# VectorE's low parts, empty-row constants and logits' running sum as instructions of one scalar and two tensors, with new emission times for all steps

## The chip, the core and the metric

The kernel runs on one core of one Trainium2 chip. A core has five engines that run side by side, each through its own queue in order: TensorE (PE in the profile; its weight loads are PEld), VectorE (DVE), ScalarE (ACT), GpSimd (POOL) and SyncE (SP), which here only issues DMA transfers. The metric is the device time of one execution in microseconds (us). The kernel before took 521.79 us (median of 3 runs, 521.64 to 521.96).

## What is computed

Attention with buckets: 4 batches of 8 heads, 768 positions, 64 dimensions a head. Each query and key gets a bucket from the signs of six projections, and a query sees only the keys of its own bucket. A mixture of experts of the soft kind follows: 32 slots, 8 experts, weights of 2 x 16.8 MB.

```python
q_bits = (np.einsum('bhsd,dk->bhsk', q, proj) > 0)
k_bits = (np.einsum('bhsd,dk->bhsk', k, proj) > 0)
mask = q_bucket[:, :, :, None] == k_bucket[:, :, None, :]
scores = np.where(mask, scale * q @ k.T, -1e9)
attn = exp(scores - max) / (sum + 1e-9)
x = attn @ v                                  # 3072 x 512
logits = x @ phi                              # 3072 x 32
d = softmax of logits over the rows           # weighs x into 32 slots
slot_out = relu(slot_input @ w1) @ w2         # four slots an expert
out = softmax of logits over the slots @ slot_out
```

A row whose query finds no key of its bucket has all scores equal, and so becomes the mean of v.

## The kernel before

The 32 heads are handled in pairs, and one pair is one period of the work. `split_hi` (ScalarE) and `split_lo` (L285, VectorE from head 4 on, GpSimd before) split queries and keys of a pair into a rounded part and the rest, the low part: low = raw - high, 128 partitions by 768, twice a pair. The parts are brought by DMA into two operands X and Y of each head (`spread_x`, `spread_y`, `spread_l`), and the sign bits, found by `bits` on TensorE and VectorE, into rows of the same operands (`spread_bits`).

For each head, `smax` multiplies twelve pieces of bits and rounded parts on TensorE into a PSUM tile of 512 columns (`smx`, two buffers), and VectorE takes the row maxima (L367, L370). The twelve pieces are of 512 and 256 columns in turn; two pieces of 256 share a tile. `shift` (L372) makes from the maxima, three small VectorE instructions one after the other, the numbers that are subtracted: L376 the maximum of a row, L377 a huge constant for rows in which nothing matches, L379 the shift itself. `shift_rows` (L383) turns them on TensorE (L386), copies them on ScalarE, and a DMA ("mr") puts them into a row of the operands. `scores` (L393) does the full product on TensorE, two matmuls a piece, into a tile of `st` (three buffers), and ScalarE takes exps into `pts` (L406). GpSimd adds these up in `acc` (five sums of 128x768 a head, L413 and L419), and `av` (L421) multiplies them with v on TensorE, 24 matmuls in a row.

For each pair, `pair_sum`, `pair_turn`, `pair_rec`, `pair_log`, `pair_add` (L461) and `pair_x` make the reciprocals of the sums, the logits and the rows of x. `pair_add` multiplies the pair's logits (L469) and adds them to a running sum over the four pairs of a batch (L471). The `batch_` steps once a batch do the softmax over rows in running form. After the last head comes the tail: the experts and the output, in which most of the weights are read.

The order of all instructions is written out in the kernel: each step has an emission time in a table, `STEADY` for what comes back every pair and `ONCE` for single steps. One unit, a slot, is a twelfth of a pair's period. The times only sort: `at` puts each step on a list with its pair's start (12 slots a pair) added, the list is sorted, and steps are emitted one after the other. Each engine, and SP's queue, then runs its part of that order; an instruction that waits holds up everything behind it on its engine. A key such as `('smax', 1, 5, 0)` names the step, the head in the pair (0 even, 1 odd) and its piece, so 14.0 in the table is slot 2.0 of the next pair. Weight pieces of 512 KB are loaded between, by `load_weights`.

Of the kernel before, what the change touches and what calls it, by code (L numbers as in the profile page):

```python
# [991 lines left out]
```

## Time and profile before

| | us |
|---|---|
| median of 3 runs | 521.79 |
| profiled execution | 522.49 |
| its span | 520.5 |
| one period (pair of heads) in the middle | 26.40 |
| tail, from 461 us on | 59.0 |

The profile shows one execution. Its first part gives the busy time of each engine and its share of the span, then come the chain of work that ended last, and the costliest groups of instructions. A group's row has the line, engine and operation, what is written from what, its shape and count, then the busy time in us, the mean of one in ns, and after the second bar how long the engine had been idle before, and what ended that. In rows of the waits stand the engine and line that waited, whom it waited for, and us in total, number of times, and the longest. In rows of the timeline stand the start and duration in us; a bracket gives the idle time before it and what ended it. Matmuls are pipelined: each is shown until its last column is out, while the next has begun, so a busy TensorE is not one at its peak.

### The profile page before, as it was taken

To read this page: it belongs to the slowest core of one execution; us is meant where nothing else is said; L and a number is where in the kernel's file an instruction comes from. 1 tells how busy PE (TensorE), PEld (TensorE's weight loads), DVE (VectorE), ACT (ScalarE), POOL (GpSimd) and SP (SyncE) were. 2 spreads that over 40 slices of the span, in tenths; PEclk is the share of its full clock that TensorE was granted. 3 is DMA by queue.
4 is the path that set the end of the run, shared out by engine and by line. 5 is a ranking of instruction groups with operands and counts; after the bars stand their busy time and mean duration, and the time that the engine had idled before them with its cause. 6 is when DMAs were issued, how large, how long until landed. Compare 5 with 4: busy or idle time off the path is not lost.

```text
span 520.5 us, 8938 instructions
## 1 busy us (share of the span) xinstructions
PE 482.5 (93%) x3155; PEld 293.3 (56%) x3155; DVE 411.6 (79%) x699; ACT 248.1 (48%) x462; POOL 336.4 (65%) x226
## 2 busy tenths in 40 slices
PE   6879899999999999999999999999999998969992
PEld 4446465656565665656555656565656565453562
DVE  4736889999998899999988999999979966544333
ACT  4044546454646464636473646464745454412232
POOL 9247859595958786867677886868678959301200
PEclk9569999999999999999999999999999999989997
DMA  3758565757565657676766676766766576779967
GB/s 104 175 104 209 152 169 140 189 124 201 117 193 117 197 123 211 151 209 151 200 156 185 169 199 169 199 168 175 188 163 173 135 206 223 290 285 369 410 270 287
DMA packets 39801, 99.60 MB, mean 191 GB/s; under 512 B 7470, under 2 KB 13756, under 8 KB 39756
## 3 DMA queue, kind: packets, MB, share of 16 engines
q1 hardware_dynamic: 38956, 97.37, 65.7%
q10 hardware_dynamic: 608, 1.57, 1.4%
q8 instruction: 25, 0.41, 0.3%
q14 instruction: 20, 0.16, 0.1%
q0 software_dynamic: 192, 0.08, 0.1%
HBM read 52.76 MB, written 6.29 MB: 113 GB/s over the span
## 4 chain that ended last, share of the span: by engine, by line
PE 78%; DVE 12%; DMA 3%; issue 2%; SPq 1%; ACT 1%; POOL 0%; DVEq 0%; POOLq 0%; ACTq 0%
PE st L402 23%; PE av L430 22%; PE smx L364 13%; DVE mz L377 4%; PE qs L915 3%; PE qh L833 3%; DVE mx L370 3%; PE mi L457 2%; PE av L237 2%; PE mi L492 2%; DVE w L287 2%; PE mi L321 2%; DMA XY<-w 2%; PE mi L386 1%; SPq L291 1%
## 5 line engine op out<-in xcount | busy, mean ns | idle before, releaser
L419 POOL TENSOR_TENSOR acc<-acc,pt 128x768 f32<-128x768 f32 x125 | 243.8, 1950 | 13.7 <-ACT pt L406 5.1
L406 ACT ACTIVATE pt<-st 128x512 f32<-128x512 f32 x288 | 166.8, 597 | 54.3 <-PE st L402 46.3
L402 PE MATMUL st<-XY 128*128 128x256 f32 (+1 forms) x768 | 184.2, 349 | 2.7 <-DMA XY<-mr 2.7
L370 DVE TENSOR_REDUCE mx<-smx 128x1 f32<-128x512 f32 x192 | 126.8, 681 | 19.5 <-PE smx L364 17.1
L402 PEld LDWEIGHTS st<-XY 128*128 128x128 f32 x768 | 124.9, 192 | 26.4 <-issue 9.0
L430 PE MATMUL av<-pt,v 128*64 128x384 f32 x768 | 130.9, 490 | 0.0
L364 PE MATMUL smx<-XY 96*128 96x512 f32 (+1 forms) x384 | 122.3, 369 | 8.7 <-DVE mx L370 3.0
L413 POOL TENSOR_TENSOR acc<-pt 128x768 f32<-128x768 f32 x32 | 58.4, 1824 | 65.3 <-ACT pt L406 64.8
L430 PEld LDWEIGHTS av<-pt,v 128*64 128x64 f32 x768 | 52.3, 137 | 76.1 <-issue 75.5
L364 PEld LDWEIGHTS smx<-XY 96*128 96x128 f32 x384 | 68.3, 194 | 30.1 <-DVE mx L370 14.6
L367 DVE TENSOR_REDUCE mx<-smx 128x2 f32<-128x512 f32 x96 | 64.4, 683 | 7.9 <-PE smx L364 7.7
L434 ACT COPY avs<-av 128x384 f32<-128x384 f32 x32 | 15.3, 479 | 113.9 <-PE av L430 113.9
L287 DVE TENSOR_TENSOR w<-raw,w 128x768 fp32r<-128x768 f32 x28 | 57.1, 2069 | 1.5 <-ACT w L283 1.5
L449 DVE RECIPROCAL sm<-sm 128x128 f32<-128x128 f32 x45 | 38.3, 907 | 0.0
L283 ACT CAST w<-raw 128x768 fp32r<-128x768 f32 x32 | 25.0, 830 | 8.7 <-DMA v<-vt 7.8
L377 DVE TENSOR_SCALAR mz<-m 128x6 f32<-128x6 f32 x32 | 25.4, 792 | 1.2
L494 DVE TENSOR_TENSOR xq<-mi,r 128x256 f32<-128x256 f32 x45 | 17.4, 414 | 6.1 <-PE mi L492 6.1
L386 PE MATMUL mi<-ident,mz 128*128 128x128 f32 x32 | 9.7, 304 | 10.9 <-DVE mz L379 10.8
L471 DVE TENSOR_TENSOR lacc<-lacc,sm 128x384 f32<-128x384 f32 x11 | 17.4, 1582 | 0.4
L386 PEld LDWEIGHTS mi<-ident,mz 128*128 128x128 f32 x32 | 4.5, 140 | 22.6 <-DVE mz L379 19.1
L389 ACT CAST mr<-mi 12x128 fp32r<-12x128 f32 x32 | 7.8, 245 | 19.5 <-PE smx L364 11.1
L492 PEld LDWEIGHTS mi<-ident,avs 128*128 128x128 f32 x90 | 10.5, 140 | 10.4 <-issue 8.4
(168 smaller groups left out, 356.7 us busy)
## 6 DMA issues: line engine op xcount, KB each, us to landing
w<-w SPq DMA_DIRECT2D x61, 512.0 KB
XY<-w SPq DMA_DIRECT2D x61, 384.0 KB
raw<-qk SPq DMA_DIRECT2D x32, 384.0 KB
XY<-w SPq DMA_DIRECT2D x60, 192.0 KB
v<-vt SPq DMA_DIRECT2D x32, 192.0 KB
out<-w SPq DMA_DIRECT2D x12, 512.0 KB
xq<-w SPq DMA_DIRECT2D x3, 512.0 KB
XY<-bt SPq DMA_DIRECT2D x62, 19.5 KB
```

The costliest lines, as they stand in the source:

```text
L283: nc.scalar.copy(w[:, 2 * x], st[h]["raw"][:, x])
L287: (nc.vector if h > 2 else nc.gpsimd).tensor_tensor(out=w[:, 2 * x + 1], in0=st[h]["raw"][:, x], in1=w[:, 2 * x], op=ALU.subtract)
L364: nc.tensor.matmul(pt[:, o:o + b - a], Ys[h % N_Y][0:96, 0, t * P:(t + 1) * P], Ys[h % N_Y][0:96, 1, a:b], start=True, stop=True)
L367: nc.vector.tensor_reduce(out=mx[:, n - 1:n + 1], in_=pt.rearrange("p (a x) -> p a x", a=2), axis=AX.X, op=ALU.max)
L370: nc.vector.reduce_max(out=mx[:, n:n + 1], in_=pt, axis=AX.X)
L377: nc.vector.tensor_scalar(out=mz[:, NT:2 * NT], in0=m, scalar1=NOMATCH, scalar2=BIG, op0=ALU.is_lt, op1=ALU.mult)
L402: nc.tensor.matmul(pt[:, o:o + b - a], x[:, 1, i * P:(i + 1) * P], x[:, 0, a:b], start=first, stop=not first)
L406: nc.scalar.activation(pts[i // 2][:, 512 * u:512 * u + 512], pt, AF.Exp, scale=D ** -0.5)
L413: nc.gpsimd.tensor_tensor(out=s["acc"], in0=pr[:, 0:S], in1=pr[:, S:2 * S], op=ALU.add)
L419: eng.tensor_tensor(out=s["acc"], in0=s["acc"], in1=pr[:, a * S:(a + 1) * S], op=ALU.add)
L430: nc.tensor.matmul(s["av"][64 * c:64 * c + 64, 0:HC], s["v"][:, i, :], pr[:, o + c * HC:o + (c + 1) * HC], start=(i == 0), stop=(i == NT - 1))
L449: nc.vector.reciprocal(out=rs[:, k * P:(k + 1) * P], in_=rs[:, k * P:(k + 1) * P])
```

## The change

Three VectorE instructions become `scalar_tensor_tensor`, which computes (in0 op0 scalar) op1 in1. The low part, a `tensor_tensor`, becomes raw x 1.0 - high for the heads where VectorE does it. The constant of empty rows, a `tensor_scalar` with two scalars, becomes (m < NOMATCH) x bigs, with `bigs` a new tile of 128x6 that holds the constant BIG and is filled once. The running sum of the logits becomes product x 1.0 + sum.

The emission times of `STEADY` are new for all steps but those of the batches, and of `ONCE` those of the weight pieces 5 to 16. The last loop's bound is written so that it takes in the last time of the plan.

```diff
@@ -43,32 +43,36 @@
 
 
 STEADY = {
-    ('acc', 0, 0): 4.9176, ('acc', 0, 1): 5.0337, ('acc', 0, 2): 6.1361, ('acc', 1, 0): 9.6777,
-    ('acc', 1, 1): 12.1046, ('acc', 1, 2): 14.8971, ('av', 0, 0): 4.8805, ('av', 0, 1): 5.7492,
-    ('av', 0, 2): 5.7838, ('av', 1, 0): 11.6706, ('av', 1, 1): 11.6874, ('av', 1, 2): 11.7943,
+    ('acc', 0, 0): 0.91143595, ('acc', 0, 1): 3.17478349, ('acc', 0, 2): 3.59676867, ('acc', 1, 0): 10.88626624,
+    ('acc', 1, 1): 11.33964379, ('acc', 1, 2): 11.82064114, ('av', 0, 0): 4.078226, ('av', 0, 1): 4.27318607,
+    ('av', 0, 2): 4.47578804, ('av', 1, 0): 11.29101187, ('av', 1, 1): 11.30451101, ('av', 1, 2): 11.80872392,
     ('batch_both',): 20.1, ('batch_exp',): 23.0, ('batch_max',): 22.4, ('batch_scale',): 24.396,
     ('batch_share',): 27.6, ('batch_slots',): 26.173, ('batch_turn',): 23.9, ('batch_weigh',): 24.65,
-    ('bits', 0): -13.9515, ('load', 0): -21.3522, ('load_v', 0): -1.8154, ('load_v', 1): 5.7068,
-    ('pair_add', 0): 17.5916, ('pair_log', 0): 16.8678, ('pair_rec', 0, 0): 16.4953, ('pair_rec', 0, 1): 17.1338,
-    ('pair_rec', 0, 2): 16.9038, ('pair_sum', 0): 15.349, ('pair_turn', 0): 16.3852, ('pair_x', 0, (0, 1)): 21.8276,
-    ('pair_x', 0, (2,)): 17.8398, ('scores', 0, 0, 0): 0.9834, ('scores', 0, 0, 1): 2.5325,
-    ('scores', 0, 1, 0): 2.9425, ('scores', 0, 1, 1): 2.5183, ('scores', 0, 2, 0): 1.1584,
-    ('scores', 0, 2, 1): -0.0074, ('scores', 0, 3, 0): 0.2266, ('scores', 0, 3, 1): 2.0502,
-    ('scores', 0, 4, 0): 3.0286, ('scores', 0, 4, 1): 3.0745, ('scores', 0, 5, 0): 3.6791,
-    ('scores', 0, 5, 1): 4.2554, ('scores', 1, 0, 0): 7.8115, ('scores', 1, 0, 1): 5.8647,
-    ('scores', 1, 1, 0): 6.6763, ('scores', 1, 1, 1): 9.4999, ('scores', 1, 2, 0): 7.9254,
-    ('scores', 1, 2, 1): 9.9037, ('scores', 1, 3, 0): 9.9177, ('scores', 1, 3, 1): 6.8119,
-    ('scores', 1, 4, 0): 7.1407, ('scores', 1, 4, 1): 8.2097, ('scores', 1, 5, 0): 9.8883,
-    ('scores', 1, 5, 1): 9.6186, ('shift', 0): -3.963, ('shift', 1): 2.6162, ('shift_rows', 0): -2.4189,
-    ('shift_rows', 1): 3.4038, ('smax', 0, 0, 0): -8.8298, ('smax', 0, 0, 1): -8.0218, ('smax', 0, 1, 0): -7.8723,
-    ('smax', 0, 1, 1): -4.9963, ('smax', 0, 2, 0): -4.1493, ('smax', 0, 2, 1): -4.8002, ('smax', 0, 3, 0): -4.4071,
-    ('smax', 0, 3, 1): -8.7934, ('smax', 0, 4, 0): -5.8528, ('smax', 0, 4, 1): -5.6775, ('smax', 0, 5, 0): -5.2739,
-    ('smax', 0, 5, 1): -7.6138, ('smax', 1, 0, 0): -2.3741, ('smax', 1, 0, 1): -3.9733, ('smax', 1, 1, 0): -3.7428,
-    ('smax', 1, 1, 1): -2.0923, ('smax', 1, 2, 0): -2.0138, ('smax', 1, 2, 1): 1.7604, ('smax', 1, 3, 0): 2.4338,
-    ('smax', 1, 3, 1): 0.8492, ('smax', 1, 4, 0): 0.923, ('smax', 1, 4, 1): -3.663, ('smax', 1, 5, 0): -2.5459,
-    ('smax', 1, 5, 1): 2.5831, ('split_hi', 0): -14.0129, ('split_lo', 0, 0): -13.788, ('split_lo', 0, 1): -12.9073,
-    ('spread_bits', 0): -10.5295, ('spread_bits', 1): -6.4877, ('spread_l', 0): -6.9257, ('spread_l', 1): -5.2234,
-    ('spread_x', 0): -9.4685, ('spread_x', 1): -5.2165, ('spread_y', 0): -13.7846, ('spread_y', 1): -7.1185,
+    ('bits', 0): -13.95890534, ('load', 0): -21.84228255, ('load_v', 0): -1.51318162, ('load_v', 1): 4.63191299,
+    ('pair_add', 0): 15.99028816, ('pair_log', 0): 15.89036858, ('pair_rec', 0, 0): 15.31234319,
+    ('pair_rec', 0, 1): 15.74808174, ('pair_rec', 0, 2): 15.83774187, ('pair_sum', 0): 14.25462034,
+    ('pair_turn', 0): 14.78228382, ('pair_x', 0, (0, 1)): 21.81002444, ('pair_x', 0, (2,)): 16.53595504,
+    ('scores', 0, 0, 0): 0.42937858, ('scores', 0, 0, 1): 0.10975419, ('scores', 0, 1, 0): 0.37566801,
+    ('scores', 0, 1, 1): 0.06354472, ('scores', 0, 2, 0): 2.73608952, ('scores', 0, 2, 1): 0.39545741,
+    ('scores', 0, 3, 0): 1.17190303, ('scores', 0, 3, 1): 2.96375079, ('scores', 0, 4, 0): 0.91043595,
+    ('scores', 0, 4, 1): 1.58215641, ('scores', 0, 5, 0): 2.32865234, ('scores', 0, 5, 1): 2.43752751,
+    ('scores', 1, 0, 0): 6.82167698, ('scores', 1, 0, 1): 5.28419876, ('scores', 1, 1, 0): 5.49659969,
+    ('scores', 1, 1, 1): 5.70056921, ('scores', 1, 2, 0): 9.5088345, ('scores', 1, 2, 1): 6.24519176,
+    ('scores', 1, 3, 0): 6.27277748, ('scores', 1, 3, 1): 9.83928317, ('scores', 1, 4, 0): 9.71651955,
+    ('scores', 1, 4, 1): 7.80253627, ('scores', 1, 5, 0): 9.44600188, ('scores', 1, 5, 1): 7.50325885,
+    ('shift', 0): -2.89738435, ('shift', 1): 2.67478786, ('shift_rows', 0): -2.14833088,
+    ('shift_rows', 1): 3.02147361, ('smax', 0, 0, 0): -7.00077299, ('smax', 0, 0, 1): -8.63468468,
+    ('smax', 0, 1, 0): -8.20918051, ('smax', 0, 1, 1): -6.29379503, ('smax', 0, 2, 0): -5.39311908,
+    ('smax', 0, 2, 1): -6.75745749, ('smax', 0, 3, 0): -6.47510133, ('smax', 0, 3, 1): -4.73315438,
+    ('smax', 0, 4, 0): -8.59086819, ('smax', 0, 4, 1): -4.27385444, ('smax', 0, 5, 0): -4.25336427,
+    ('smax', 0, 5, 1): -3.26636443, ('smax', 1, 0, 0): 2.40118286, ('smax', 1, 0, 1): -2.02963968,
+    ('smax', 1, 1, 0): -2.01736929, ('smax', 1, 1, 1): 0.30153939, ('smax', 1, 2, 0): 0.03611274,
+    ('smax', 1, 2, 1): 1.34851447, ('smax', 1, 3, 0): 1.74922724, ('smax', 1, 3, 1): 2.09633042,
+    ('smax', 1, 4, 0): 2.28076515, ('smax', 1, 4, 1): -2.41700748, ('smax', 1, 5, 0): -2.06779907,
+    ('smax', 1, 5, 1): 0.84522444, ('split_hi', 0): -14.12691859, ('split_lo', 0, 0): -13.3249754,
+    ('split_lo', 0, 1): -13.04048452, ('spread_bits', 0): -13.92314133, ('spread_bits', 1): -8.21018051,
+    ('spread_l', 0): -4.89960371, ('spread_l', 1): -6.85974162, ('spread_x', 0): -10.40239078,
+    ('spread_x', 1): -7.05038, ('spread_y', 0): -11.52688803, ('spread_y', 1): -8.46779598,
 }
 
 ONCE = {
@@ -78,24 +82,24 @@
...
-    ('load_weights', 14): 129.5946, ('load_weights', 15): 135.9087, ('load_weights', 16): 141.5946,
...
-    ('load_weights', 5): 75.9087, ('load_weights', 6): 81.5946, ('load_weights', 7): 87.9087,
...
+    ('load_weights', 13): 118.272186073, ('load_weights', 14): 124.277596692, ('load_weights', 15): 130.272186073,
+    ('load_weights', 16): 136.277596692, ('load_weights', 17): 153.5946, ('load_weights', 18): 156.8062,
...
+    ('load_weights', 4): 63.9087, ('load_weights', 5): 70.272186073, ('load_weights', 6): 76.277596692,
...
@@ -195,6 +199,8 @@
 
     eps = cp.tile([P, 1], F32, name="eps")
     nc.vector.memset(eps, EPS)
+    bigs = cp.tile([P, NT], F32, name="bigs")
+    nc.vector.memset(bigs, BIG)
     ones = cp.tile([P, 32], F32, name="ones")
     nc.vector.memset(ones, 1.0)
     idle = pts[2][:, 0:P]
@@ -284,7 +290,12 @@
 
     def split_lo(h, x):
         w = st[h]["w4"]
-        (nc.vector if h > 2 else nc.gpsimd).tensor_tensor(out=w[:, 2 * x + 1], in0=st[h]["raw"][:, x], in1=w[:, 2 * x], op=ALU.subtract)
+        raw = st[h]["raw"][:, x]
+        if h > 2:
+            nc.vector.scalar_tensor_tensor(out=w[:, 2 * x + 1], in0=raw, scalar=1.0, in1=w[:, 2 * x],
+                                           op0=ALU.mult, op1=ALU.subtract)
+        else:
+            nc.gpsimd.tensor_tensor(out=w[:, 2 * x + 1], in0=raw, in1=w[:, 2 * x], op=ALU.subtract)
 
     def move(dst, src, eng=nc.sync):
 
@@ -374,8 +385,8 @@
         mz = mzp
         m = mp.tile([P, NT], F32, name="m", bufs=1)
         nc.vector.tensor_reduce(out=m, in_=s["mx"], axis=AX.X, op=ALU.max)
-        nc.vector.tensor_scalar(out=mz[:, NT:2 * NT], in0=m, scalar1=NOMATCH, scalar2=BIG,
-                                op0=ALU.is_lt, op1=ALU.mult)
+        nc.vector.scalar_tensor_tensor(out=mz[:, NT:2 * NT], in0=m, scalar=NOMATCH, in1=bigs,
+                                       op0=ALU.is_lt, op1=ALU.mult)
         nc.vector.scalar_tensor_tensor(out=mz[:, 0:NT], in0=m, scalar=-1.0, in1=mz[:, NT:2 * NT],
                                        op0=ALU.mult, op1=ALU.subtract)
         s["mz"] = mz
@@ -468,7 +479,8 @@
             dst = st[h]["rs"]
         nc.vector.tensor_tensor(out=dst, in0=pt[:, 0:HC], in1=st[h]["rs"], op=ALU.mult)
         if g:
-            nc.vector.tensor_tensor(out=lacc_of[b], in0=lacc_of[b], in1=dst, op=ALU.add)
+            nc.vector.scalar_tensor_tensor(out=lacc_of[b], in0=dst, scalar=1.0, in1=lacc_of[b],
+                                           op0=ALU.mult, op1=ALU.add)
 
     def pair_turn(h):
         sm = st[h]["sm"]
@@ -773,7 +785,7 @@
         at(load_weights, wa, 1, tag=n)
 
     plan.sort(key=lambda w: w[:2])
-    for slot in range(int(plan[0][0] // 1), last + 5):
+    for slot in range(int(plan[0][0] // 1), max(last + 5, int(plan[-1][0]) + 1)):
         if slot == last - 14:
             free_pp()
             wb = ctx.enter_context(tc.tile_pool(name="wb", bufs=N_WB))
```

More of the change, by code (lines that the diff above doesn't have):

```diff
@@ L85 @@
-    ('load_weights', 2): 39.9087, ('load_weights', 20): 168.8062, ('load_weights', 21): 177.5946,
-    ('load_weights', 22): 189.5946, ('load_weights', 3): 51.9087, ('load_weights', 4): 63.9087,
-    ('load_weights', 5): 75.9087, ('load_weights', 6): 81.5946, ('load_weights', 7): 87.9087,
-    ('load_weights', 8): 93.5946, ('load_weights', 9): 99.9087, ('one_add', 30): 190.708, ('one_add', 31): 193.725,
-    ('one_fold', 3): 189.992, ('one_log', 30): 188.431, ('one_log', 31): 193.725, ('one_put', 30): 192.78,
@@ L90 @@
-    ('one_put', 31): 195.725, ('one_rec', 30): 190.438, ('one_rec', 31): 193.725, ('one_sum', 30): 189.395,
-    ('one_sum', 31): 193.725, ('one_turn', 30): 189.777, ('one_turn', 31): 193.725, ('one_x', 30): 191.23,
-    ('one_x', 31): 193.725, ('smax', 1, 0, 0): -2.3, ('smax', 1, 0, 1): -2.29, ('smax', 1, 1, 0): -2.28,
-    ('smax', 1, 1, 1): -2.1, ('smax', 1, 2, 0): -2.05, ('smax', 1, 2, 1): -2.0, ('smax', 1, 3, 0): -1.99,
-    ('smax', 1, 3, 1): -1.9, ('smax', 1, 4, 0): -1.8, ('smax', 1, 4, 1): 0.62, ('smax', 1, 5, 0): 0.63,
@@ L95 @@
-    ('smax', 1, 5, 1): 1.2, ('split_hi', 2): -1.5, ('split_lo', 2, 0): -1.45, ('split_lo', 2, 1): -1.44,
-    ('spread_bits', 1): -7.869, ('spread_bits', 2): 0.4, ('spread_l', 0): -12.047, ('spread_l', 1): -12.02,
-    ('spread_l', 2): 0.5, ('spread_x', 0): -12.04, ('spread_x', 1): -12.03, ('spread_x', 2): 0.6,
-    ('spread_y', 1): -14.012, ('spread_y', 2): -1.2,
+    ('load_phi',): -7.0, ('load_weights', 0): 16.4515, ('load_weights', 1): 27.9087,
+    ('load_weights', 10): 100.277596692, ('load_weights', 11): 106.272186073, ('load_weights', 12): 112.277596692,
@@ new lines @@
+    ('load_weights', 13): 118.272186073, ('load_weights', 14): 124.277596692, ('load_weights', 15): 130.272186073,
+    ('load_weights', 16): 136.277596692, ('load_weights', 17): 153.5946, ('load_weights', 18): 156.8062,
+    ('load_weights', 19): 165.5946, ('load_weights', 2): 39.9087, ('load_weights', 20): 168.8062,
+    ('load_weights', 21): 177.5946, ('load_weights', 22): 189.5946, ('load_weights', 3): 51.9087,
+    ('load_weights', 4): 63.9087, ('load_weights', 5): 70.272186073, ('load_weights', 6): 76.277596692,
@@ new lines @@
+    ('load_weights', 7): 82.272186073, ('load_weights', 8): 88.277596692, ('load_weights', 9): 94.272186073,
+    ('one_add', 30): 190.708, ('one_add', 31): 193.725, ('one_fold', 3): 189.992, ('one_log', 30): 188.431,
+    ('one_log', 31): 193.725, ('one_put', 30): 192.78, ('one_put', 31): 195.725, ('one_rec', 30): 190.438,
+    ('one_rec', 31): 193.725, ('one_sum', 30): 189.395, ('one_sum', 31): 193.725, ('one_turn', 30): 189.777,
+    ('one_turn', 31): 193.725, ('one_x', 30): 191.23, ('one_x', 31): 193.725, ('smax', 1, 0, 0): -2.3,
@@ new lines @@
+    ('smax', 1, 0, 1): -2.29, ('smax', 1, 1, 0): -2.28, ('smax', 1, 1, 1): -2.1, ('smax', 1, 2, 0): -2.05,
+    ('smax', 1, 2, 1): -2.0, ('smax', 1, 3, 0): -1.99, ('smax', 1, 3, 1): -1.9, ('smax', 1, 4, 0): -1.8,
+    ('smax', 1, 4, 1): 0.62, ('smax', 1, 5, 0): 0.63, ('smax', 1, 5, 1): 1.2, ('split_hi', 2): -1.5,
+    ('split_lo', 2, 0): -1.45, ('split_lo', 2, 1): -1.44, ('spread_bits', 1): -7.869, ('spread_bits', 2): 0.4,
+    ('spread_l', 0): -12.047, ('spread_l', 1): -12.02, ('spread_l', 2): 0.5, ('spread_x', 0): -12.04,
@@ L99 @@
+    ('spread_x', 1): -12.03, ('spread_x', 2): 0.6, ('spread_y', 1): -14.012, ('spread_y', 2): -1.2,
 }
```

3 lines of the change are left out of this document (removed).

## The prediction

> **What bounds the kernel now.** I read the page first, then the table of windows, the waits, and the timeline of one period. The page:
>
> ```profile
> span 520.5 us, 8938 instructions
> PE 482.5 (93%) x3155; PEld 293.3 (56%) x3155; DVE 411.6 (79%) x699; ACT 248.1 (48%) x462; POOL 336.4 (65%) x226
> PE 78%; DVE 12%; DMA 3%; issue 2%; SPq 1%; ACT 1%; POOL 0%; DVEq 0%; POOLq 0%; ACTq 0%
> ```
>
> TensorE is busy 93% and makes 78% of the chain that ended last; VectorE's 12% is what can be taken out. One period is two heads, 12 slots of the plan. Its row in the table of windows:
>
> ```profile
> core 0: us, PE busy (x) PEld busy (x) DVE busy (x) ACT busy (x) POOL busy (x), PEclk, DMA share, GB/s
> 112.70:139.10 26.40, 25.48 (x156) 15.74 (x156) 24.90 (x37) 13.82 (x26) 19.44 (x11) 1.00 0.63 161
> ...
> 461.00:520.00 59.00, 49.46 (x547) 28.68 (x547) 21.36 (x75) 15.59 (x34) 6.03 (x32) 0.93 0.82 323
> ```
>
> In 26.40 us TensorE stands still for 0.92 us, at full clock; VectorE is busy for 24.90. The last row, the tail, is little touched by the change. The waits name the standstill, and the timeline shows one:
>
> ```profile
> PE mi L386 <- DVE mz L379: 10.8, 12, 1.3
> ```
>
> ```profile
> 113.66 0.69 DVE L370 TENSOR_REDUCE mx<-smx 128x1 f32<-128x512 f32 x1 [0.23 <-PE smx L364]
> ...
> 114.38 0.17 DVE L376 TENSOR_REDUCE m<-mx 128x6 f32<-128x12 f32 x1
> ...
> 114.57 1.81 POOL L413 TENSOR_TENSOR acc<-pt 128x768 f32<-128x768 f32 x1 [0.19 <-ACT pt L406]
> 114.58 1.83 DVE L377 TENSOR_SCALAR mz<-m 128x6 f32<-128x6 f32 x1
> ...
> 116.45 0.17 DVE L379 SCALAR_TENSOR_TENSOR mz<-m,mz 128x6 f32<-128x6 f32 x1
> 116.46 7.53 POOL L419 TENSOR_TENSOR acc<-acc,pt 128x768 f32<-128x768 f32 x4
> ...
> 116.67 0.33 PE L386 MATMUL mi<-ident,mz 128*128 128x128 f32 x1 [0.86 <-DVE mz L379]
> ```
>
> L377 handles six numbers per partition, yet begins 0.01 us after GpSimd's sum and ends just when that ends. Such a standstill happens in 12 of 32 heads and costs TensorE 10.8 us in all. The other VectorE rows that the change touches:
>
> ```profile
> L287 DVE TENSOR_TENSOR w<-raw,w 128x768 fp32r<-128x768 f32 x28 | 57.1, 2069 | 1.5 <-ACT w L283 1.5
> ...
> L377 DVE TENSOR_SCALAR mz<-m 128x6 f32<-128x6 f32 x32 | 25.4, 792 | 1.2
> ...
> L471 DVE TENSOR_TENSOR lacc<-lacc,sm 128x384 f32<-128x384 f32 x11 | 17.4, 1582 | 0.4
> ...
> L379 DVE SCALAR_TENSOR_TENSOR mz<-m,mz 128x6 f32<-128x6 f32 x32 | 5.3, 166 | 1.1
> ...
> L419 DVE TENSOR_TENSOR acc<-acc,pt 128x768 f32<-128x768 f32 x2 | 1.9, 950 | 0.0
> ...
> L648 DVE SCALAR_TENSOR_TENSOR run_x<-run_x,al,mi 128x512 f32<-128x512 f32 x2 | 1.5, 746 | 3.7 <-PE mi L642 3.7
> ...
> L922 DVE SCALAR_TENSOR_TENSOR w<-w,con,qs 128x256 fp32r<-128x256 f32 x2 | 1.0, 480 | 5.9 <-ACT w L921 5.9
> ...
> L555 DVE TENSOR_TENSOR lacc<-lacc,sm 64x384 f32<-64x384 f32 x1 | 0.6, 551 | 0.0
> ```
>
> A two-tensor sum of 768 columns takes 950 ns where GpSimd does nothing (L419 on VectorE) and 2069 ns as L287, where GpSimd sums. Of 384 columns it is 551 against 1582. So more than half of L287 and L471, and four fifths of L377, is waiting for GpSimd.
>
> **The new instructions.** A two-tensor, one-scalar instruction with both tensors in SBUF and 768 columns isn't in this trace. The rows of that form, L922 and L648 (one tensor in PSUM), give (746 - 480) / 256 = 1.04 ns a column, the rate of the two-tensor form ((950 - 551) / 384 = 1.04). So without a wait a low part costs about 1.0 us, the running sum 0.6, the empty-row constant 0.17 (as L379). The other end is the wait that stands now, 2.07, 1.58 and up to 1.83, and on top of it a second pass over the columns, 768 x 1.04 = 0.8. L379 has both tensors in SBUF and never took more than its 0.17, but in the row shown it began 0.01 before GpSimd, so it cannot decide. I take the lower end, the rows of the same form, and keep the upper as rivals. Per period VectorE then loses 2 x (2.07 - 1.0) + 2 x (0.79 - 0.17) + (1.58 - 0.6) = 4.4 us of 24.90. That alone gives nothing: only what TensorE waits for counts.
>
> **What the new times do.** Steps are listed by their time modulo 12, those of a next pair's even head shifted by 12. TensorE's costs are from these rows:
>
> ```profile
> 114.96 0.85 PE L442 MATMUL mi<-acc,ones 128*32 128x384 f32 x8
> ...
> 118.07 0.49 PE L477 MATMUL mi<-ident,sm 128*128 128x128 f32 x3
> ...
> 119.50 4.09 PE L430 MATMUL av<-pt,v 128*64 128x384 f32 x24
> ...
> 127.62 0.28 PE L364 MATMUL smx<-XY 96*128 96x256 f32 x1
> ...
> 137.29 1.10 PE L402 MATMUL st<-XY 128*128 128x512 f32 x4
> ```
>
> Four matmuls of 512 columns end after 1.10, one ends after 0.40: each further one is (1.10 - 0.40) / 3 = 0.23; of 256 columns half that, 0.12, and of 128 0.11 (three transposes take 0.49, so pair_turn costs 0.33). A row maximum is one matmul, a scores part two.
>
> Before, the last row maximum ahead of the odd head's shift is smax(1,5,1) at 2.58; then come, on TensorE, three scores parts, two row maxima and pair_sum up to shift_rows at 3.40: 0.24 + 0.47 + 0.24 + 0.23 + 0.23 + 0.85 = 2.3 us of cover. VectorE needs 0.2 to see the maximum's tile, 0.69 for it, 0.6 for the three shift instructions, 3.2 with the 1.66 of waiting: 0.9 short, as the row says.
>
> After, the last one is smax(1,0,0) at 2.40, and up to shift_rows at 3.02 stand scores(0,5,1), (0,2,0), pair_turn and (0,3,1): 0.47 + 0.47 + 0.33 + 0.47 = 1.7 us. VectorE needs 0.2 + 0.69 + 0.6 = 1.5, and has some 0.2 of backlog from the two maxima at 2.10 and 2.28: cover and need are equal. GpSimd is out of the way there: the four scores parts that acc(0,0) sums move from between 0.98 and 2.94 to between 0.06 and 0.43, so its 1.8 us are over before the shift, and acc(0,1) needs scores(0,2,0) and (0,3,1) at 2.74 and 2.96, which come behind it. So the wait at this place goes with either form of L377. For the even head, shift 9.10 (was 8.04) and shift_rows 9.85 (was 9.58) have four scores parts, a row maximum and four transposes between them, 0.24 + 3 x 0.47 + 0.12 + 0.44 = 2.2 us against 1.5.
>
> The low parts stay at the end of the period, under the 4.09 us of av. Behind av comes smax(1,2,0) at 0.04, whose maximum VectorE must take before TensorE's third maximum from there, about 2 us on: that is the cover of late low parts. Rows of the place:
>
> ```profile
> 131.79 1.56 ACT L283 CAST w<-raw 128x768 fp32r<-128x768 f32 x2
> 132.04 8.74 POOL L419 TENSOR_TENSOR acc<-acc,pt 128x768 f32<-128x768 f32 x4 [0.44 <-ACT pt L406]
> 132.22 4.09 PE L430 MATMUL av<-pt,v 128*64 128x384 f32 x24
> 132.97 4.20 DVE L287 TENSOR_TENSOR w<-raw,w 128x768 fp32r<-128x768 f32 x2
> ```
>
> With 2.0 instead of 4.20 they end before av does; GpSimd's four sums shrink from 8.74 to the 7.53 of the row at 116.46. Without this gain they end about 1 us behind av, inside the cover.
>
> Moved transfers: spread_y of the even head goes from -1.78 to 0.47 of the period, and its first row maximum stands at 3.37, 2.9 slots (6 us) on; spread_bits of the even head goes from 1.47 to -1.92, right behind bits, so its four issues wait on SP for VectorE's bits with load_v, spread_y and spread_x queued behind, which all have slots to spare; spread_l of the even head goes behind the odd head's transfers (5.07 to 7.10). SP issues them in a row of some 8 us behind the odd head's mr transfer, and the next split_hi waits for the last to land. Rows from the first period give the time from issue to that:
>
> ```profile
> 46.31 2.16 SPq L291 DMA_DIRECT2D XY<-w  x3
> ...
> 52.63 1.57 ACT L283 CAST w<-raw 128x768 fp32r<-128x768 f32 x2 [1.47 <-DMA v<-vt]
> 53.55 4.89 DVE L287 TENSOR_TENSOR w<-raw,w 128x768 fp32r<-128x768 f32 x2 [1.17 <-ACT w L283]
> ...
> 59.10 0.39 PE L364 MATMUL smx<-XY 96*128 96x256 f32 x1 [1.38 <-DVE mx L370]
> ```
>
> Some 4 us after the last issue. In the new order that makes split_hi up to 1 us later than its place on ScalarE, which the shorter low parts cover. The weight loads 5 to 16 move about 6 slots earlier at the same spacing: nothing. The memset of bigs is beside the first loads: nothing.
>
> **The sum,** against the profiled execution's 522.49 us (span 520.5): 12 stalls at L386, 10.8; the stall at 59.10 behind 4.89 us of low parts, 1.4; and the short waits for row maxima, of which this is one of a period's two:
>
> ```profile
> 117.27 0.30 PEld L364 LDWEIGHTS smx<-XY 96*128 96x128 f32 x2 [0.24 <-DVE mx L370]
> ```
>
> They end inside matmuls that count as busy and cost some 0.2 each, 14 periods x 0.4 = 5.6, of which I take a third, 1.9, since the new order will have its own. Together 14.1, which makes a period 25.3. The profiled execution is 0.70 above the median, and the gain is the same there: 521.79 - 14.1 = 507.7, say **508**. Without any gain in the short waits it is 510, with all of it and no new ones 504.
>
> **Rivals.**
>
> *The instructions wait as before.* For: L287 reads two SBUF tensors, and so will its successor. Then 2.07 and 1.58 stay, L377's successor may wait too, and only the order gains: low parts 1 us behind av, about 0.4 us a period of new waits at row maxima: 508 + 14 x 0.4 = 514. The Trainium skill, "SBUF — State Buffer", section "Who interferes with whom", states this rule for any VectorE instruction with two SBUF inputs; by it the sum would be this rival's, and the rows of L287 and L471 agree for the two-tensor form, while none here shows the other form at that length.
>
> *They wait and also take a second pass.* This ends on the other side. Low parts of 2.07 + 0.8 are 5.7 us a period, and GpSimd is held up by them 1.6 longer, which moves the next low part too: they end 3.3 us behind av, against 2 us of cover. From 2 us on each further one is a stall: 1.3, and 0.4 from the running sum, so 25.3 + 1.7 = 27.0 a period against 26.40, 14 x 0.6 = 8 slower: 530. The Trainium skill, "Vector Engine (DVE) Microarchitecture Reference", section "Points that are easy to get wrong", has it that this form with two SBUF sources that aren't bf16 runs at half throughput. Without the wait, 1.8 a low part ends inside av's cover, and the forecast stands.
>
> *The new order has a wait in place of the old.* The cover of the odd head's shift is 1.7 against 1.5 and a backlog; if VectorE is later by half a microsecond, TensorE waits 0.5 in each of 14 periods: 508 + 7 = 515.
>
> **How the numbers follow.** Forecast 0.62 (504 to 511); waiting as before 0.17 (510 to 517); a new wait in the order 0.12 (511 to 521); waiting and a second pass 0.09 (522 to 533). Leaving out the last and a little on each side, the range is 503 to 518. A measurement of this kernel can tell 0.2%, 1.0 us, from no change. Faster takes the first two and most of the third, 0.87; same 0.04; slower 0.09.
>
> **What would show it.** Right: no row for L386 waiting on L379's successor; periods of about 25.2 in the table of windows; low parts near 1.0 us while GpSimd sums stay at 1.83. If low parts show 1.8 with GpSimd undisturbed, the second pass is real and the wait gone; if 1.7 to 2.6, they wait as before. Wrong: a period over 26, with TensorE waiting for row maxima behind the low parts, for spread_y or for ScalarE's exps.

## The result, and the profile after

| | before | changed |
|---|---|---|
| median, first measurement (us) | 521.71 (521.08 to 521.96) | 525.29 (524.37 to 525.80) |
| ratio | | 1.0068, 95% interval 1.0051 to 1.0086 |
| median, second measurement, another chip (us) | 521.28 (519.59 to 525.02) | 522.20 (520.37 to 527.43) |
| ratio | | 1.0012, 95% interval 0.9983 to 1.0041 |
| profiled execution / its span (us) | 522.49 / 520.5 | 524.37 / 522.6 |

The first measurement has the changed kernel slower by 0.7%, the second can't tell it from the kernel before; 508 us was predicted, and no measurement has it faster. Ratios, and the medians of the experiments, leave out single runs that took over 1.5% longer than the fastest of their kernel. Lines have moved: the low part L287 is now L295, the row maximum L370 is L381, the empty-row constant L377 is L388, the shift's transpose L386 is L397, the running sum L471 is L482. The page of the changed kernel:

```profile
span 522.6 us, 9003 instructions
...
PE 482.3 (92%) x3155; PEld 295.6 (57%) x3155; DVE 396.8 (76%) x700; ACT 245.6 (47%) x462; POOL 331.8 (63%) x226
...
PE 63%; DVE 14%; DMA 12%; SPq 5%; issue 3%; ACT 1%; DVEq 0%; ACTq 0%
```

TensorE's work is the same (482.3 against 482.5), so the 2.1 us that the span grew by are standstill. VectorE is busy 14.8 us less, and yet its share of the chain rose; DMA and SP's queue went from 4% to 17% of it. One period and the tail, in the table of windows:

```profile
118.10:144.80 26.70, 25.40 (x161) 15.77 (x157) 23.13 (x38) 13.70 (x25) 19.05 (x11) 1.00 0.62 160
463.00:522.00 59.00, 49.51 (x547) 28.70 (x545) 21.33 (x75) 15.62 (x33) 6.03 (x32) 0.94 0.81 319
```

The period is 26.70 us, with 1.30 us of standstill, where it had 0.92; the tail is as it was. The waits, first two rows of the changed kernel, then two of the kernel before:

```profile
PE smx L375 <- DVE mx L381: 18.8, 19, 1.6
...
PE st L413 <- DMA XY<-mr: 2.3, 1, 2.3
```

```profile
PE mi L386 <- DVE mz L379: 10.8, 12, 1.3
...
PE smx L364 <- DVE mx L370: 3.0, 7, 1.4
```

No row is left for L397 behind L390: the old standstill is gone. Another took its place, TensorE in front of a piece of `smx` whose tile VectorE hasn't read: 18.8 us instead of 3.0. So 10.8 went and 15.8 came; the other rows shrank by some 2.2. VectorE's groups:

```profile
L295 DVE SCALAR_TENSOR_TENSOR w<-raw,w 128x768 fp32r<-128x768 f32 x28 | 60.3, 2192 | 22.8 <-ACT w L289 17.1 <-DMA XY<-bt 5.6
...
L482 DVE SCALAR_TENSOR_TENSOR lacc<-sm,lacc 128x384 f32<-128x384 f32 x11 | 17.9, 1627 | 0.4
...
L388 DVE SCALAR_TENSOR_TENSOR mz<-m,bigs 128x6 f32<-128x6 f32 x32 | 6.9, 214 | 1.2
```

The low part takes 2192 ns (2069 before), the running sum 1627 (1582): nothing was saved there. Only the empty-row constant fell, from 792 to 214. And VectorE now stands idle for 17.1 us ahead of low parts, waiting for ScalarE's high parts (L289). One period's timeline shows why; SPq is SP's queue, whose rows say when a transfer was issued and how long the issuing took:

```profile
117.62 0.83 SPq L302 DMA_DIRECT2D XY<-mr  x1
...
118.06 4.09 PE L441 MATMUL av<-pt,v 128*64 128x384 f32 x24
...
118.56 0.65 SPq L302 DMA_DIRECT2D XY<-w  x1
...
119.25 4.17 SPq L302 DMA_DIRECT2D XY<-bt  x4
...
123.47 0.52 SPq L180 DMA_DIRECT2D w<-w  x1
...
124.04 0.42 SPq L279 DMA_DIRECT2D v<-vt  x1
...
124.57 4.28 SPq L302 DMA_DIRECT2D XY<-w  x4
...
130.38 4.09 PE L441 MATMUL av<-pt,v 128*64 128x384 f32 x24
...
132.53 1.56 ACT L289 CAST w<-raw 128x768 fp32r<-128x768 f32 x2 [2.53 <-DMA XY<-w]
...
133.39 4.09 DVE L295 SCALAR_TENSOR_TENSOR w<-raw,w 128x768 fp32r<-128x768 f32 x2 [2.08 <-DMA XY<-bt]
...
137.41 1.97 DVE L381 TENSOR_REDUCE mx<-smx 128x1 f32<-128x512 f32 x3
...
138.14 0.50 PE L375 MATMUL smx<-XY 96*128 96x512 f32 x1 [1.30 <-DVE mx L381]
```

The tile that holds the split parts has one buffer. ScalarE may write the next pair's high parts into it only when the last transfer that reads the old parts (the `XY<-w x4`, issued up to 128.85) has landed. The trace has that landing at 132.28, and ScalarE, which had stood idle for 2.53 us, begins at 132.53. By then the av of the odd head (`av(1)`) has run for 2.15 us. The low parts end at 137.48, 3.0 us behind av, and TensorE waits 1.30 us for the maximum behind them. In the prediction's rows of the kernel before, the high parts began 0.43 us ahead of that av (131.79 against 132.22). They did not wait for a transfer there: the last one had landed at 131.04, and they came right behind exps on ScalarE.

### The profile page after: what moved, and what is told of

The parts are those of the page before. It is cut to its first block, busy times and chain, and to the rows that moved or that the text cites. A ratio compares the mean times of both kernels' runs of the same rounds, so it can differ in the third digit from the quotient of the medians.

```text
span 522.6 us, 9003 instructions
## 1 busy us (share of the span) xinstructions
PE 482.3 (92%) x3155; PEld 295.6 (57%) x3155; DVE 396.8 (76%) x700; ACT 245.6 (47%) x462; POOL 331.8 (63%) x226
## 4 chain that ended last, share of the span: by engine, by line
PE 63%; DVE 14%; DMA 12%; SPq 5%; issue 3%; ACT 1%; DVEq 0%; ACTq 0%
PE st L413 17%; PE av L441 15%; PE smx L375 11%; DMA XY<-w 7%; DVE w L295 7%; SPq L302 5%; DMA XY<-bt 4%; PE qs L927 3%; PE qh L845 3%; PE av L243 2%; PE mi L468 2%; PE mi L453 2%; DVE mx L381 2%; PE mi L504 2%; DVE mx L378 2%
## 5 line engine op out<-in xcount | busy, mean ns | idle before, releaser
L430 POOL TENSOR_TENSOR acc<-acc,pt 128x768 f32<-128x768 f32 x125 | 239.8, 1919 | 72.0 <-ACT pt L417 64.5
L413 PE MATMUL st<-XY 128*128 128x512 f32 (+1 forms) x768 | 179.1, 347 | 2.3 <-DMA XY<-mr 2.3
L375 PE MATMUL smx<-XY 96*128 96x256 f32 (+1 forms) x384 | 127.4, 382 | 22.6 <-DVE mx L381 18.8
L381 DVE TENSOR_REDUCE mx<-smx 128x1 f32<-128x512 f32 x192 | 128.1, 680 | 15.8 <-PE smx L375 15.1
L413 PEld LDWEIGHTS st<-XY 128*128 128x128 f32 x768 | 127.7, 192 | 18.2 <-issue 4.2
L295 DVE SCALAR_TENSOR_TENSOR w<-raw,w 128x768 fp32r<-128x768 f32 x28 | 60.3, 2192 | 22.8 <-ACT w L289 17.1
L289 ACT CAST w<-raw 128x768 fp32r<-128x768 f32 x32 | 25.0, 830 | 36.9 <-DMA XY<-w 14.8
L460 DVE RECIPROCAL sm<-sm 128x128 f32<-128x128 f32 x45 | 41.2, 919 | 0.0
L482 DVE SCALAR_TENSOR_TENSOR lacc<-sm,lacc 128x384 f32<-128x384 f32 x11 | 17.9, 1627 | 0.4
L504 PEld LDWEIGHTS mi<-ident,avs 128*128 128x128 f32 x90 | 10.4, 140 | 10.9 <-issue 9.0
L298 POOL TENSOR_TENSOR w<-raw,w 128x768 fp32r<-128x768 f32 x4 | 7.2, 1806 | 13.8 <-ACT w L289 13.8
L504 PE MATMUL mi<-ident,avs 128*128 128x128 f32 x90 | 15.6, 282 | 0.0
L927 PE MATMUL qs<-w 128*32 128x256 f32 x232 | 15.2, 382 | 0.0
```

What stands on the lines that cost most here:

```text
L295: nc.vector.scalar_tensor_tensor(out=w[:, 2 * x + 1], in0=raw, scalar=1.0, in1=w[:, 2 * x], op0=ALU.mult, op1=ALU.subtract)
L375: nc.tensor.matmul(pt[:, o:o + b - a], Ys[h % N_Y][0:96, 0, t * P:(t + 1) * P], Ys[h % N_Y][0:96, 1, a:b], start=True, stop=True)
L381: nc.vector.reduce_max(out=mx[:, n:n + 1], in_=pt, axis=AX.X)
L413: nc.tensor.matmul(pt[:, o:o + b - a], x[:, 1, i * P:(i + 1) * P], x[:, 0, a:b], start=first, stop=not first)
L430: eng.tensor_tensor(out=s["acc"], in0=s["acc"], in1=pr[:, a * S:(a + 1) * S], op=ALU.add)
L460: nc.vector.reciprocal(out=rs[:, k * P:(k + 1) * P], in_=rs[:, k * P:(k + 1) * P])
```

## The experiments

Each edit is against the changed kernel unless said otherwise; "before" is the kernel before on the same chip.

### The two halves of the change

`e1_new_times_old_forms` has the new emission times and the three old instructions; `e2_old_times_new_forms` the reverse.

```diff
# e1: the three instructions as they were
-            nc.vector.scalar_tensor_tensor(out=w[:, 2 * x + 1], in0=raw, scalar=1.0, in1=w[:, 2 * x],
-                                           op0=ALU.mult, op1=ALU.subtract)
+        (nc.vector if h > 2 else nc.gpsimd).tensor_tensor(out=w[:, 2 * x + 1], in0=st[h]["raw"][:, x], in1=w[:, 2 * x], op=ALU.subtract)
...
# e2: STEADY and ONCE as they were
```

> The new emission times with the three VectorE instructions in their old forms. Theory A (order): the slowdown comes from the times alone, since the new form waits for GpSimd just as the old one (low parts 1.0 to 2.6 us in both), and what is late is ScalarE's split_hi, behind the transfers that free its tile: 525 us, within 1.5 of the changed kernel, periods of 26.7, low parts that end some 3 us behind av. Theory B (forms): the new form is slower or holds the port longer and eats what the order gains: 510 to 520 us, periods of 25.4 to 26.2.

> The old emission times with the three new forms. Theory A: the same waits as before, the constant of empty rows 1.83 us in 12 heads, TensorE's wait at the transpose of the shift 0.86 us, 521.7 us within 1.5. Theory B: 524 us or more if the form itself is slower. If the form does escape GpSimd (the prediction's view): the wait goes and 509 to 513.

e1: 522.97 us, ratio 1.0026 (1.0007 to 1.0045). e2: 521.72 us, ratio 0.9981 (0.9945 to 1.0018). The instructions alone do nothing, and the new times alone bring no gain. Rows of e2, the groups and a wait:

```profile
L291 DVE SCALAR_TENSOR_TENSOR w<-raw,w 128x768 fp32r<-128x768 f32 x28 | 56.0, 2030 | 0.8 <-ACT w L285 0.8
...
L384 DVE SCALAR_TENSOR_TENSOR mz<-m,bigs 128x6 f32<-128x6 f32 x32 | 25.2, 787 | 1.2
```

```profile
PE mi L393 <- DVE mz L386: 10.7, 12, 1.3
```

In the old order the new form of the six-column constant waits just as the old did (787 against 792 ns), and TensorE behind it 10.7 us in 12 places. With old forms and new times (e1) no such wait of TensorE is left, and the old form of the constant (L381 in e1's numbering) takes 214 ns there, as the new one does in the changed kernel:

```profile
L381 DVE TENSOR_SCALAR mz<-m 128x6 f32<-128x6 f32 x32 | 6.8, 214 | 1.2
```

So the order removed the wait, not the form.

The changed kernel and e1 had been measured on different chips and lay 0.4% apart. They were run again side by side:

> The changed kernel once more, beside e14_new_times_old_forms_again on one chip. It was 0.68% slower than before in its own measurement, and e1_new_times_old_forms 0.26%, on different chips. Theory (the forms cost nothing): the two kernels within 0.2% of each other, both 0.2 to 0.7% slower than before. Rival (the new forms cost some 2 us in the new order): this one 0.3 to 0.5% slower than the other.

> The new times with the old forms once more, beside e13_changed_again. Theory: the same time as that within 0.2%. Rival: 0.3 to 0.5% faster than that.

522.20 us, ratio 1.0012 (0.9983 to 1.0041), and 522.67 us, ratio 1.0015 (0.9991 to 1.0039): the same. The forms cost nothing and bring nothing in either order, and on this chip the loss against before is too small to be told from none.

### Does the low part wait for GpSimd, and does that matter?

```diff
         if j == 0:
             s["acc"] = accs[h % 3]
-            nc.gpsimd.tensor_tensor(out=s["acc"], in0=pr[:, 0:S], in1=pr[:, S:2 * S], op=ALU.add)
-        else:
+            if h < 3:
+                nc.gpsimd.memset(s["acc"], 1.0)
+        elif h == BH - 1:
```

> The changed kernel with GpSimd's five sums a head left out: each head's acc is a constant tile, so reciprocals and output are other numbers. Transfers and their order are those of the changed kernel, so the high parts are as late as there. Theory (two causes are needed, high parts 2.5 us late and low parts that wait for GpSimd): low parts take 0.95 us each instead of 2.19, end within 1 us behind av, TensorE no longer waits 1.3 us for the row maximum of L381; periods of 25.3, 508 to 512. Rival (the late transfers alone are enough): low parts are short but the row maxima still come late, periods of 26.3 or more, 521 to 525.

504.21 us, ratio 0.9638 (0.9601 to 0.9676), even below the 508 to 512 expected. Groups of VectorE and one period, in the table of windows:

```profile
L295 DVE SCALAR_TENSOR_TENSOR w<-raw,w 128x768 fp32r<-128x768 f32 x28 | 25.6, 955 | 21.2 <-ACT w L289 21.1
...
L482 DVE SCALAR_TENSOR_TENSOR lacc<-sm,lacc 128x384 f32<-128x384 f32 x11 | 6.1, 558 | 0.4
```

```profile
118.00:143.00 25.00, 25.00 (x157) 15.82 (x156) 19.98 (x38) 13.70 (x25) 0.00 (x0) 1.00 0.67 170
```

With GpSimd silent the same instruction takes 955 ns instead of 2192, and the running sum 558 instead of 1627. That is the lower end of the prediction (1.0 and 0.6 us). So there is no second pass over the columns, and 1.24 us of each low part is waiting. The high parts come as late as in the changed kernel (VectorE is idle 21.1 us for them), but the low parts end by 0.2 to 0.9 us behind av and TensorE doesn't stand still in this period; its wait for L381 is 1.6 us in all. The edit also frees other instructions of VectorE, such as the running sum, so not all of the gain is the low parts'. But lateness alone isn't enough; it takes the wait for GpSimd as well.

### What makes the high parts late

```diff
# e3, and e12 the same again
-    ('spread_l', 0): -4.89960371,
+    ('spread_l', 0): -10.35,
```

> The changed kernel with one time altered: the even head's spread_l goes right behind its spread_x instead of behind the odd head's transfers. Theory A: the last transfer that reads the split tile is issued 0.7 to 1 us sooner, split_hi and the low parts start as much sooner, TensorE's wait behind av falls from 1.3 to about 0.5 us: 14 periods x 0.8 = 11 off 525, 514 (511 to 520). Theory B: 525, nothing.

> The kernel of e3_low_rows_early once more, beside the other three on one chip, since the runs of the kernel before scattered from 519.6 to 525.8 on the chip used last. Theory: faster than before by 1.2 to 1.8% again. Rival (its first measurement was a lucky chip): within 0.5% of before.

e3: 514.76 us, ratio 0.9849 (0.9788 to 0.9911); e12: 515.11 us, ratio 0.9862 (0.9807 to 0.9917). This beats the kernel before, and on e3's chip also e1 (522.97), the new times with old forms. The even head's low rows are now issued ahead of the odd head's mr transfer. A period of e3:

```profile
114.63 0.83 SPq L302 DMA_DIRECT2D XY<-mr  x1
...
121.09 2.66 SPq L302 DMA_DIRECT2D XY<-w  x3
...
127.37 4.09 PE L441 MATMUL av<-pt,v 128*64 128x384 f32 x24
...
128.18 1.57 ACT L289 CAST w<-raw 128x768 fp32r<-128x768 f32 x2 [1.19 <-DMA XY<-w]
...
129.04 3.51 DVE L295 SCALAR_TENSOR_TENSOR w<-raw,w 128x768 fp32r<-128x768 f32 x2 [0.73 <-ACT w L289]
```

```profile
115.06:140.24 25.18, 25.18 (x160) 15.86 (x156) 22.60 (x38) 13.71 (x25) 19.70 (x11) 1.00 0.66 172
```

```profile
PE st L413 <- DMA XY<-mr: 8.7, 7, 2.4
...
PE smx L375 <- DVE mx L381: 4.6, 7, 1.6
```

The high parts begin 0.81 us behind av's start, the low parts end 1.09 us behind its end, TensorE stands still for nothing in this period, and the wait for L381 falls from 18.8 to 4.6 us. A period of 25.18 is what the prediction had (25.3). But another wait has grown, for the mr transfer, from 2.3 to 8.7.

Is it the place of the low rows among the transfers, or the number of issues between the mr transfer and the last read of the split tile? In `e8_low_rows_halfway` the low rows go between the odd head's bits and its x and low rows. In `e5_raw_load_later` the low rows are early as in e3, but the two raw loads of the next pair are put behind the mr transfer. `e7_e5_old_forms` is e5 with the old instructions.

```diff
# e8
-    ('spread_l', 0): -4.89960371,
+    ('spread_l', 0): -7.5,
# e5, against e3
-    ('load', 0): -21.84228255,
+    ('load', 0): -20.90,
```

> The changed kernel with the even head's spread_l at slot 4.5, behind the odd head's y and bits but ahead of its x and low rows (changed kernel: behind all of them, slot 7.10; e3_low_rows_early: ahead of all, slot 1.65). Theory (the time follows the moment at which the split tile is free): between the two, high parts some 1 us earlier than in the changed kernel, the wait for L381 at about half, 517 to 522. Rival (only the extremes matter, through the queueing of the odd head's bits transfers): as the changed kernel, 524 to 526, or as e3_low_rows_early, 514 to 516.

> e3_low_rows_early with the next pair's two raw transfers (0.77 MB) emitted behind the odd head's mr transfer (slot 3.10 instead of 2.16). In the trace of e3_low_rows_early the scores wait 8.7 us in 7 places for mr transfers that were issued right behind the raw ones. Theory (mr queues behind raw): these waits go, the later raw still lands some 10 us before split_hi needs it, time about 508 to 510 where e3_low_rows_early has 514.8. Rival (mr is late because of the weight pieces and the queue as a whole, not because of raw): the waits stay, 513 to 516. Other rival: raw now lands too late for the high parts, split_hi waits for it, 518 or more.

> e5_raw_load_later with the three old instruction forms. Theory (the forms do nothing, since both wait for GpSimd alike): same time as e5_raw_load_later within 0.2%, low parts of 1.9 to 2.2 us in both. Rival (the new forms are worth some 2 us, the difference between the changed kernel and e1_new_times_old_forms, 525.3 against 523.0, with its sign reversed in the better order): 1 to 2 us faster or slower.

e8: 522.90 us, ratio 1.0013 (0.9984 to 1.0043), no gain for half the way: its high parts came 1.4 to 3.5 us behind the start of av(1), no earlier than in the changed kernel (1.4 to 2.3). e5: 523.43 us, ratio 1.0015 (0.9993 to 1.0038), a miss: the whole gain of e3 was gone. e7: 522.86 us, ratio 1.0008 (0.9986 to 1.0031), as e5. The row of the page that e5 was made for, and its period:

```profile
L413 PE MATMUL st<-XY 128*128 128x512 f32 (+1 forms) x768 | 179.4, 347 | 1.6 <-DMA XY<-mr 1.5
```

```profile
115.26 0.83 SPq L302 DMA_DIRECT2D XY<-mr  x1
...
123.60 2.89 SPq L302 DMA_DIRECT2D XY<-w  x3
...
128.01 4.09 PE L441 MATMUL av<-pt,v 128*64 128x384 f32 x24
...
131.05 1.57 ACT L289 CAST w<-raw 128x768 fp32r<-128x768 f32 x2 [3.42 <-DMA XY<-bt]
```

The wait for mr did go (1.5 us, from 8.7), so raw close ahead of mr makes mr late. But the raw issues now stand in the stretch that decides. The row of the high parts names a transfer of bits as what ended their wait; the profile infers that. The trace has the last `XY<-w` landing at 130.79, 0.26 us ahead of the high parts, and that distance is 0.25 in the changed kernel (132.28) and in e3 (127.93), so this landing is the likelier end of the wait. The raw parts had landed at 121.37, so they were not late themselves. The same stretch of the kernel before, in its timeline:

```profile
117.31 0.81 SPq L291 DMA_DIRECT2D XY<-mr  x1
...
124.97 2.16 SPq L291 DMA_DIRECT2D XY<-w  x3
```

From such rows, for one period of each kernel (high parts and av of before from the prediction's rows):

| us | mr issue to av(1) | mr issue to end of last issue | from there to high parts | high parts behind start of av(1) |
|---|---|---|---|---|
| before | 14.91 | 9.82 | 4.66 | -0.43 |
| changed | 12.76 | 11.23 | 3.68 | +2.15 |
| e3 | 12.74 | 9.12 | 4.43 | +0.81 |
| e5 | 12.75 | 11.23 | 4.56 | +3.04 |

In the row of before the 4.66 is no landing time, since the high parts did not wait: the last transfer landed 3.91 us behind the last issue.

The new order issues the odd head's mr transfer 0.44 us ahead of the even head's av (117.62 against 118.06), where it was 2.19 (117.31 against 119.50), and SP's issues behind it took 1.4 us longer. Both make the high parts later. The low rows stood in that stretch before as well (between y and the bits), so their place in it is nothing, as e8 says; taking them out of it (e3) is worth 2.1 us. Put together over the periods between 100 and 330 us:

| kernel | low parts end behind av (us) | TensorE's wait for L381, or L370 (us) |
|---|---|---|
| before | 0.86 to 0.94 | 3.0 |
| changed | 3.01 to 3.14 | 18.8 |
| e3 | 1.07 to 1.26 | 4.6 |
| e5 | 2.85 to 3.27 | 16.5 |
| e8 | 3.02 to 3.27 | 17.0 |
| e6, GpSimd silent | 0.17 to 0.93 | 1.6 |

In these periods nothing lies between 1.3 and 2.8. From 60 us on, in all runs with the new times and GpSimd's sums but e4, the jump lies at one place. Where the high parts began up to 1.07 us behind the start of av(1), the low parts ended at most 1.30 us behind its end in 67 of 68 periods; where they began 1.09 us or more behind it, at least 2.85 us in all 88. (In e4 two periods of 13 with early high parts end 2.2 and 2.4 us behind av.) Instruction by instruction, 27 of the 28 low parts of the changed kernel end 0.82 us after one of GpSimd's sums has ended, and the sum beside them takes some 2.44 us instead of 1.83: they take turns, and low parts that miss one end a sum later. That fits the jump of 1.9; that it alone makes the jump was not tried.

### The mr transfer on ScalarE's queue

```diff
# e10; e9 is the same with e3's place of spread_l
-        move(XYs[h % N_Y][ROW:ROW + 1, 0].rearrange("o y (t p) -> o (y t) p", p=P), mr)
+        move(XYs[h % N_Y][ROW:ROW + 1, 0].rearrange("o y (t p) -> o (y t) p", p=P), mr, nc.scalar)
```

> The changed kernel with that one edit: mr transfers issued by ScalarE's DMA queue, spread_l where the change has it. Theory (the loss is made by SP's chain from the odd head's mr wait to the last read of the split tile, 11.2 us long, and not by the low rows' place as such): the chain starts without waiting for mr, high parts come 2 us or more earlier, low parts end about 1 us behind av instead of 3.0, TensorE's 18.8 us of waits for L381 mostly go; time 508 to 514. Rival (the bits of the odd head or the data themselves are what is late): high parts as in the changed kernel, 523 to 526.

> e3_low_rows_early with the mr transfers issued by ScalarE's DMA queue, right behind ScalarE's own copy, instead of SP's. In e3_low_rows_early SP stands 49.4 us waiting for ScalarE's mr copies with the spread transfers queued behind it, and the scores wait 8.7 us for mr transfers queued behind raw. Theory (one queue, in order, is what makes both late): both waits go, ScalarE pays some 0.8 us more a head and has room (busy 47%); the high parts are at or ahead of their place in every period; time 507 to 511. Rival (the mr data are slow because all queues share the transfer engines): waits for mr stay, 513 to 516. Other rival: the exps are delayed by the issues on ScalarE and TensorE waits for st: 517 or more.

e10: 518.34 us, ratio 0.9939 (0.9895 to 0.9984), less of a gain than the 508 to 514 expected. With SP's queue no longer held by the wait for mr, the low parts end 1.03 to 1.27 us behind av in seven of the nine periods between 100 and 330 us and the wait for L381 falls to 5.9 us, with the low rows where the change has them: the theory of the stretch holds. Waits for mr eat much of the gain, 10.4 us in the profiled execution of 523.45 us, 5 us above that median:

```profile
PE st L413 <- DMA XY<-mr: 10.4, 9, 2.5
...
PE smx L375 <- DVE mx L381: 5.9, 8, 1.8
```

e9: 526.67 us, ratio 1.0147 (1.0055 to 1.0239), a miss. A period of e9, where ACTq is ScalarE's own queue:

```profile
110.51 1.66 SPq L191 DMA_DIRECT2D raw<-qk  x2
...
112.46 0.73 ACTq L302 DMA_DIRECT2D XY<-mr  x1
...
120.43 1.22 PE L413 MATMUL st<-XY 128*128 128x256 f32 x4 [2.67 <-DMA XY<-mr]
```

The mr transfer has 6 KB, was alone on its queue and issued at 113.19; the matmul had it at 120.43, 7.2 us on. So it isn't SP's queue that holds mr up. The packets in the trace point to the data of other transfers: the last of mr's twelve packets of 512 bytes started at 119.19, 2.9 us behind the one before it, straight after packets of 3 KB of other transfers and one of 16 KB of instructions (118.18 to 119.20), and the landing came at 120.38. The Trainium skill, "DMA: Bandwidth & Descriptors", section "Issuing engines are not separate DMA queues", says that transfers issued by any engine run on the same 16 DMA engines and interleave there; this row agrees.

### Two versions that went further

```diff
# e4, against e3: the odd head's x and low rows ahead of its bits
-    ('spread_l', 1): -6.85974162, ('spread_x', 1): -7.05038,
+    ('spread_l', 1): -8.38, ('spread_x', 1): -8.40,
# e11, against e3: v and the even weight pieces behind the odd head's x and low rows
-    ('load_v', 1): 4.63191299, ('load_weights', 10): 100.277596692,
+    ('load_v', 1): 5.22, ('load_weights', 10): 101.258,
```

> As the run before, and the odd head's spread_x and spread_l are also issued ahead of its four bit transfers. Theory A: the split tile is free some 6 us sooner, split_hi starts right behind the shift's copy on ScalarE (2.5 us sooner than in the changed kernel), the low parts end 1 us behind av, inside TensorE's cover: periods of 25.4 to 25.6, 508 us (504 to 513); the odd head's bits land 2 us later, and if its first row maximum waits for them, up to 1 us a period is lost again (522). Theory B: 522 to 525.

> e3_low_rows_early with the odd head's v transfer and the even-numbered weight pieces 6 to 16 moved behind the odd head's x and low rows (slots 5.22 and 5.26 instead of 4.63 and 4.28), so that SP's chain ahead of the split tile's release is about 1.1 us shorter. Theory (lateness costs only beyond a cover of about 2 us behind av, and e3_low_rows_early is at 1.1): the high parts come up to 1 us earlier, the time stays within 0.3% of e12_low_rows_early_again on the same chip. Rival (each microsecond of the chain counts, as e3_low_rows_early's own gain of 2.1 us in each of 14 periods might suggest): another 5 us or more faster.

e4: 529.13 us, ratio 1.0118 (1.0060 to 1.0176), a miss: the split tile is free in time, but the bits and the mr transfer come late, and TensorE waits 8.4 us for mr and 6.1 for bits. e11: 521.37 us, ratio 0.9979 (0.9941 to 1.0017). The high parts did come earlier, ahead of av in all but one period, and the low parts end 0.3 to 1.2 us behind it: no gain from that, as the theory has it, since e3 was already inside the cover. But the time wasn't that of e3's kernel, as expected (515.11 in e12, on the same chip), but 6 us more. In the profiled execution of 524.27 us, 3 us above the median, av waits 6.0 us for v; how much of the 6 us that makes stays open.

## Why the prediction was wrong

**Right.** The standstill of 10.8 us at L386 went, by the order alone. A period without a standstill has 25.18 us (25.3 predicted; its 14.1 us over 14 periods would make that 25.4). The cover behind av was put at 2 us: at 1.1 us TensorE doesn't wait, at 3.0 it waits 1.30, so it is 1.7. There is no second pass: 955 ns for 768 columns is the rate of the two-tensor form, so the rival that ended at 530 is out. The half throughput that the Trainium skill has for this form ("Vector Engine (DVE) Microarchitecture Reference", section "Points that are easy to get wrong") is not seen here.

**Wrong, first step: "I take the lower end, the rows of the same form".** The rows that I took, L922 and L648, have one tensor in PSUM; the new instructions have both in SBUF, as L287 had, and waited as L287 did: 2192 ns instead of 1000. The rival "the instructions wait as before" was true in this. The nearest row was the one with the same places of its operands, not the one with the same name. The Trainium skill's rule that was cited for the rival ("SBUF — State Buffer", section "Who interferes with whom") held, for this form too: 955 ns alone, 2192 beside GpSimd.

**Wrong, second step: "that makes split_hi up to 1 us later than its place on ScalarE, which the shorter low parts cover".** The time from the last issue to the high parts was about right (some 4 us; 3.68 measured). The rest was not: SP's row of issues was put at 8 us and took 11.2 from the issue of mr on, and that mr is issued 2.15 us closer to av(1) was not counted. Both were in the trace or in the list of times. The high parts stood 2.53 us behind their place on ScalarE in the period shown, and 1.8 to 2.7 us in 12 of the 13 periods from 60 us on, where 1 us was allowed for; against av they came 2.6 us later than before. One microsecond would have put them 0.6 us behind the start of av(1), ahead of the jump at 1.07 to 1.09. And the cover named for it, shorter low parts, was the gain of the first step.

**Where the two met.** "Without this gain they end about 1 us behind av, inside the cover" was worked out for high parts in time, as e3 shows (1.09). The rivals were priced one by one, at 514 and 515. Together they make a standstill of 1.30 us in place of 0.92 in the period shown. The sum of both was never made: low parts that end 0.9 us behind av as before, and high parts 2.6 us later, are 3.5 us against 2 of cover (3.0 measured).

**The size.** The prediction's gain was 14.1 us. e3, the order without its late high parts, gains 7: its good periods have the 25.18, but its waits for mr take 8.7 us, which the prediction had left at the 2.7 of the kernel before, and behind two of them the clock fell (below).

## What to carry to other kernels

Price an instruction by the row whose operands lie in the same memories, not by the row with the same operation. When an order is changed, follow the queue of transfers as one more engine: list its issues between the event that it waits for and the last one that frees a buffer, and compare the sum with the room that is left. Price rivals together where one takes away the cover that the other needs.
